# 64-token chunks, values scaled in place of keys, and a new order of all pieces in a fused RetNet and channel-mix kernel

## The chip, the cores and the metric

The kernel runs on one core of one Trainium2 chip. The metric is the device time of that core in microseconds (us), the median of several runs. The core's engines run side by side, each through its own queue in order: TensorE (PE in the profile, with its weight loads as PEld), VectorE (DVE), ScalarE (ACT), GpSimd (POOL) and SyncE (SP). DMAs are issued from SP, ACT and POOL; only those issued from POOL change the type on the way in this kernel.

## The reference

Four sequences of 768 tokens go through a recurrence with 8 heads of 64 channels, and its output x (512 channels) through an RWKV channel mix with a hidden width of 1024:

```python
gamma = 1.0 - 2.0 ** (-5.0 - np.arange(H))
for t in range(S):
    state = gamma[None, :, None, None] * state + np.einsum('bhd,bhe->bhde', k[:, :, t], v[:, :, t])
    y[:, :, t] = scale * np.einsum('bhd,bhde->bhe', q[:, :, t], state)
...
xk = mu_k * x + (1.0 - mu_k) * x_prev          # x_prev: x one token earlier
xr = mu_r * x + (1.0 - mu_r) * x_prev
k = np.maximum(xk @ w_k, 0.0)
v = k * k @ w_v
r = 1.0 / (1.0 + np.exp(-(xr @ w_r)))
return (r * v).astype(np.float32)
```

## The kernel before

A block is 256 tokens of one sequence; there are 12 blocks, three to a sequence (n = 0 to 11). The recurrence is computed in chunks of 128 tokens, two to a block. Within a block a chunk is held on 64 partitions, each with two neighbouring tokens (i = 0, 1), so one row of a load is 128 numbers of 4 bytes. The decay is taken out: keys are multiplied by powers of gamma (`scale_k`, L191, on DVE or POOL), scores are masked with a 0/1 matrix, and the result is multiplied by `gy` (`yout`, L343), a table that `powers` (L503, L506) makes.

Per block the pieces are: loads of k, q, v (L178; q and v are made 16-bit on the way); `ks`, the scaling of keys; T, Tq, Tk, the transposes on PE (L206, L224), and E, their copies out of PSUM on ACT (L252); S, the scores (L260), and M, the mask on DVE (L267, once for each i); C, the chunk's share of the state (L285); U, its sum with the decayed state (L297, L301), and G, the decay of that sum on POOL (L304); I and Y, the product of state and queries and that of scores and values (L316, L329); D, `gy` (L343, L351); dx, the difference of neighbouring tokens (L358, on DVE or POOL); X, the two mixes xk and xr, four pieces each (L372). Then K, the matmuls with w_k (L389, L409), with Q, relu and square on ACT (L397 to L419); R, the gate's matmuls (L423), and s, its sigmoid on ACT (L429); V, the matmuls with w_v (L435, the last block's second half in two parts, L453); O, the product (L441, L460); st, the store (L448). z are matmuls on zeros that fill PE's time at the start (L497).

The order is written out by hand or by a program, as one text of words, `ORDER`. A word is a piece with its numbers and, behind @, its PSUM banks; each engine gets its instructions in the order of the words. The framework puts in the waits. Buffers are rings of two to six tiles; a load waits until the last reader of the tile four blocks back has finished. In the first two blocks several pieces are split (Xu, du, Du, Ku work on 128 tokens).

```python
out=KS(n)[:, :, h0:h1], in0=K32(n)[:, h0:h1].rearrange("p h (i d) -> p i h d", i=2),
in1=gks[:, :, h0:h1, None].to_broadcast([P, 2, h1 - h0, D]), op=ALU.mult
```

Of the kernel before, what the change touches and what calls it, by code (L numbers as in the profile page):

```python
# [14 lines left out]
KSC = 64.0  # L15
ORDER = """
lk.0.0.2.4 lk.0.0.0.2 lq.0.0.2 lq.0.2.4 lv.0 lk.1.2 lq.1 ks.0.0.2.4 lv.1 wk.0 ks.0.0.0.2 gy z.12@1
T.0.1.0.2@0 wk.1 T.0.1.2.4@1 E.0.1.0.2 lk.2.2 mu z.2@4 Tq.0.2.4@23 Tq.0.0.2@45 E.0.0.0.2 E.0.1.2.4
z.3@6 S.0.0.0.2@45 C.0@67 M.0.0.0.2 E.0.0.2.4 U.0.0 z.1@0 S.0.0.2.4@23 M.0.0.2.4 I.0.0@45
S.0.1.0.2@01 ks.1.1 M.0.1.0.2 z.1@6 S.0.1.2.4@23 M.0.1.2.4 U.0.1 z.4@6 Y.0 G.0.1 Tq.1@67 Du.0.1  # L20
T.1.1@2 E.1.0 lq.2 Du.0.0 mt@3 wr me du.0.0.1 E.1.1 du.0.0.0 wv.0 Xu.0.1.1.1.2 z.6@0 S.1.0@23 lv.2
Xu.0.0.0.3.4 C.1@45 Xu.0.0.1.3.4 Xu.0.0.0.2.3 Xu.0.0.0.0.1 wv.1 Xu.0.0.1.1.2 Xu.0.0.0.1.2
Xu.0.1.1.0.1 lq.3 Xu.0.1.1.2.3 z.6@0 Ku.0.0.0@6 Xu.0.0.1.0.1 Xu.0.0.1.2.3 lk.3.2 Xu.0.1.1.3.4
Ku.0.1.0@7 Xu.0.1.0.2.3 Qu.0.0.0 U.1.0 M.1.0 G.1.0 Ku.0.0.1@4 Qu.0.1.0 ks.2.1 I.1.0@01 S.1.1@67
M.1.1 Tq.2@23 Xu.0.1.0.1.2 Y.1 E.2.0 Xu.0.1.0.3.4 U.1.1 T.2.1@6 Du.1.0 G.1.1 Qu.0.0.1 Ku.0.1.1@7
lk.4.2 du.1.0.0 R.0.1@0 Xu.0.1.0.0.1 Qu.0.1.1 lv.3 Xu.1.0.0.0.1 Xu.1.0.0.2.3 Xu.1.0.0.3.4 R.0.0@7
Xu.1.0.0.1.2 lv.4 E.2.1 Du.1.1 Ku.1.0.0@4 Xu.1.1.0.0.1 s.0.0 du.1.0.1 lq.4 V.0.1.0@1 Qu.1.0.0
Xu.1.1.0.1.2 Xu.1.1.1.0.1 Xu.1.1.0.2.3 lk.5.2 S.2.0@45 Xu.1.1.1.3.4 C.2@7 Xu.1.0.1.2.3
Xu.1.1.0.3.4 Ku.1.1.0@6 Xu.1.0.1.3.4 U.2.0 M.2.0 R.1.0@2 G.2.0 Qu.1.1.0 V.0.0.0@3 lv.5
Xu.1.1.1.2.3 s.0.1 s.1.0 I.2.0@45 S.2.1@67 V.0.0.1 M.2.1 V.0.1.1 Xu.1.0.1.0.1 Xu.1.0.1.1.2 ks.3.1  # L30
Y.2 O.0.1 Tq.3@67 O.0.0 Ku.1.0.1@2 D.2 lk.6.2 Ku.1.1.1@3 Qu.1.0.1 dx.2.0 lq.5 T.3.1@2 Qu.1.1.1
V.1.0.0@4 X.2.0.2.3 V.1.1.0@3 E.3.1 X.2.0.1.2 X.2.0.0.1 ks.4.0 V.1.0.1 E.3.0 C.3@01 Xu.1.1.1.1.2
lk.8 S.3.0@67 X.2.0.3.4 T.4.1@2 X.2.1.1.2 K.2.1@5 O.1.0 E.4.1 U.3.0 X.2.1.3.4 K.2.0@4 Q.2.1
X.2.1.0.1 X.2.1.2.3 R.1.1@5 U.3.1 Q.2.0 M.3.0 G.3.1 V.1.1.1 s.1.1 C.4@01 O.1.1 I.3.0@45 S.3.1@67
R.2.0@2 M.3.1 st.1.1 st.0.1 K.2.2@3 st.0.0 s.2.0 U.4.0 st.1.0 G.4.0 Tq.4@67 Y.3 ks.5.1 E.4.0 U.4.1
V.2.1.0@2 D.3 Q.2.2 S.4.0@67 I.4.0@01 dx.3.1 S.4.1@45 lk.9 M.4.0 K.2.3@3 M.4.1 R.2.1@6 Q.2.3 G.4.1
V.2.0.0@3 lq.6 X.3.1.0.1 s.2.1 X.3.1.1.2 V.2.0.1 X.3.0.3.4 lv.7 X.3.0.1.2 Tk.5@67 X.3.0.0.1 lq.7
Tq.5@45 X.3.1.3.4 E.5.1 V.2.1.1 X.3.1.2.3 lv.6 X.3.0.2.3 E.5.0 R.3.1@6 O.2.0 lq.8 O.2.1 C.5@3
S.5.0@45 U.5.0 Y.4 G.5.0 R.3.0@7 D.4 ks.6.1 K.3.3@3 s.3.0 M.5.0 s.3.1 K.3.1@2 Q.3.3 lv.8 dx.4.0
I.5.0@45 S.5.1@67 lk.7.2 Q.3.1 K.3.0@3 M.5.1 lq.9 K.3.2@2 Q.3.0 X.4.0.1.2 lk.10.2 ks.8.0 Tk.6@67  # L40
Y.5 Q.3.2 V.3.0.0@3 D.5 E.6.1 V.3.1.0@2 X.4.0.3.4 X.4.1.3.4 V.3.1.1 dx.5.0 C.6@67 Tq.7@45
X.4.1.2.3 Tq.6@01 X.4.0.0.1 E.7.0 V.3.0.1 X.4.0.2.3 X.4.1.1.2 E.6.0 K.4.2@4 U.6.0 O.3.0 K.4.0@6
X.4.1.0.1 Q.4.2 st.3.0 X.5.0.3.4 st.2.1 O.3.1 S.6.0@45 Tk.8@01 Q.4.0 X.5.1.1.2 st.3.1 K.4.1@3
X.5.0.1.2 E.8.1 X.5.1.2.3 R.4.0@6 X.5.0.0.1 X.5.1.3.4 X.5.0.2.3 K.4.3@2 s.4.0 X.5.1.0.1 Q.4.1
ks.7.0 K.5.1@6 Q.4.3 R.5.1@3 U.6.1 lk.11 M.6.0 G.6.1 st.2.0 V.4.0.0@7 s.5.1 ks.9.1 Q.5.1 V.4.0.1
Tk.7@45 O.4.0 I.6.0@23 S.6.1@01 E.7.1 K.5.2@6 M.6.1 C.7@45 Q.5.2 Y.6 U.7.0 S.7.0@67 G.7.0 D.6
Tq.8@01 V.4.1.0@4 E.8.0 lv.10 dx.6.0 V.4.1.1 lq.11 R.4.1@0 X.6.0.1.2 U.7.1 K.5.0@1 s.4.1 M.7.0
G.7.1 lq.10 K.5.3@0 Q.5.0 O.4.1 lv.9 X.6.0.2.3 Tq.9@67 I.7.0@45 Q.5.3 X.6.1.2.3 S.7.1@23 X.6.1.3.4
R.5.0@1 X.6.0.0.1 X.6.1.0.1 V.5.0.0@0 s.5.0 X.6.0.3.4 M.7.1 E.9.0 V.5.0.1 K.6.1@1 O.5.0 X.6.1.1.2
S.8.0@23 Q.6.1 Y.7 Tk.9@01 D.7 C.8@6 E.9.1 K.6.2@7 dx.7.0 R.6.1@4 K.6.3@5 X.7.0.3.4 X.7.1.0.1  # L50
R.6.0@0 Q.6.3 X.7.0.0.1 X.7.1.1.2 K.6.0@5 U.8.0 s.6.1 M.8.0 G.8.0 V.5.1.0@6 Q.6.0 ks.10.1 I.8.0@45
S.8.1@23 Q.6.2 V.5.1.1 M.8.1 s.6.0 lv.11 V.6.0.0@7 X.7.0.1.2 O.5.1 S.9.0@01 C.9@23 X.7.1.3.4
st.5.1 Y.8 X.7.1.2.3 st.5.0 X.7.0.2.3 st.4.1 V.6.0.1 U.9.0 st.4.0 D.8 K.7.3@2 M.9.0 dx.8.1 R.7.0@6
Q.7.3 V.6.1.0@2 O.6.0 s.7.0 U.9.1 I.9.0@01 S.9.1@67 G.9.1 K.7.0@3 M.9.1 K.7.1@4 Q.7.0 X.8.1.0.1
X.8.0.2.3 V.6.1.1 X.8.1.2.3 Q.7.1 X.8.1.1.2 Y.9 X.8.0.0.1 Tq.10@45 D.9 Tk.10@67 K.7.2@3 X.8.0.1.2
R.7.1@0 X.8.0.3.4 Q.7.2 dx.9.0 K.8.1@3 X.9.0.3.4 K.8.0@1 Q.8.1 X.9.1.1.2 X.8.1.3.4 V.7.1.0@3 O.6.1
E.10.0 V.7.1.1 X.9.1.2.3 st.6.1 X.9.0.2.3 Q.8.0 ks.11.0 K.8.2@2 E.10.1 V.7.0.0@1 X.9.0.0.1
X.9.0.1.2 s.7.1 V.7.0.1 Q.8.2 O.7.1 K.8.3@0 O.7.0 st.7.0 C.10@23 Q.8.3 S.10.0@67 st.7.1 U.10.0
Tk.11@45 st.6.0 M.10.0 Tq.11@01 G.10.0 V.8.0.0@2 E.11.0 U.10.1 E.11.1 I.10.0@67 G.10.1 S.10.1@01
R.8.0@3 M.10.1 V.8.1.0@4 s.8.0 X.9.1.3.4 X.9.1.0.1 C.11@3 S.11.0@01 U.11.0 Y.10 M.11.0 G.11.0  # L60
V.8.1.1 D.10 R.9.1@3 I.11.0@01 dx.10.1 s.9.1 S.11.1@67 K.9.1@5 M.11.1 R.8.1@3 Q.9.1 X.10.0.1.2
X.10.1.0.1 Y.11 s.8.1 X.10.1.1.2 X.10.0.3.4 R.9.0@5 X.10.1.3.4 X.10.0.2.3 K.9.0@3 X.10.1.2.3
X.10.0.0.1 K.9.2@6 Q.9.0 D.11 V.8.0.1 O.8.1 K.9.3@3 dx.11.0 K.10.3@4 X.11.1.1.2 K.10.0@7
X.11.1.3.4 X.11.0.2.3 X.11.0.1.2 V.9.1.0@0 Q.10.0 O.8.0 V.9.0.0@7 X.11.0.0.1 st.8.0 Q.9.3
X.11.0.3.4 X.11.1.2.3 R.10.1@1 X.11.1.0.1 Q.9.2 R.10.0@3 s.9.0 K.10.1@6 Q.10.3 V.9.1.1 s.10.1
K.10.2@2 Q.10.1 O.9.1 K.11.1@6 st.9.1 st.8.1 K.11.2@0 Q.11.1 V.10.1.0@6 Q.10.2 R.11.0@1 Q.11.2
V.10.1.1 s.10.0 K.11.3@0 O.10.1 s.11.0 K.11.0@3 st.10.1 V.10.0.0@1 Q.11.0 V.10.0.1 Q.11.3 V.9.0.1
O.10.0 V.11.0.0@6 st.10.0 O.9.0 V.11.0.1 st.9.0 R.11.1@7 O.11.0 st.11.0 Vc.11.1.0@6 s.11.1
Vc.11.1.1@7 Oc.11.1.0 sc.11.1.0.0 Oc.11.1.1 sc.11.1.1.1
# [4 lines left out]
def kernel(  # L74
# [17 lines left out]
    C = 128  # L92
    TM = 2 * C
# [6 lines left out]
    LOG = 7  # L100
# [3 lines left out]
    tok = 2 * (par % (P // 2))[:, None] + np.arange(2)[None, :]  # L104
    causal_np = (np.arange(C)[None, None, :] >= tok[:, :, None]).astype(np.float16)
    c16_np = np.concatenate([np.eye(P, dtype=np.float16), causal_np.reshape(P, -1)], axis=1)
    gk_np = gam[None, None, :] ** (C - 1 - tok[:, :, None])
    h_pj = 2 * np.arange(NJ)[None, :] + (par // D)[:, None]
    gd_np = gam[h_pj] ** C
    g0_np = 0.125 * KSC * gam[h_pj] ** (1 - C)  # L110
    pw_np = gam[h_pj][:, None, :] ** (2.0 ** np.arange(LOG)[None, :, None])
    small_np = np.concatenate(
        [x.reshape(P, -1) for x in (gk_np, gd_np, g0_np, pw_np, np.eye(P, 2 * NCO))], axis=1
    ).astype(np.float32)
    c16d = nc.inline_tensor(c16_np, name="c16")
    smalld = nc.inline_tensor(small_np, name="csmall")

# [9 lines left out]
    V16 = ring("v16_", 4, [H, 2 * D], F16)  # L127
    K32 = ring("k32_", 4, [H, 2 * D], F32)
    KS = ring("ks_", 3, [2, H, D], F16)
    QT = ring("qT_", 3, [NJ, 2, C], F16)  # L130
    KT = ring("kT_", 3, [NJ, 2, C], F16)
    A2 = ring("a2_", 3, [2, 2, NJ, C], F16)
    T32 = ring("t32_", 4, [NJ, D], F32)
    TG = ring("tg_", 6, [NJ, D], F16)
    DX = ring("dx_", 2, [NJ, TM], F32)
    XM = [ring("xk_", 3, [NJ, TM], F16), ring("xr_", 3, [NJ, TM], F16)]
    KR = ring("kr_", 2, [2, TM], F32)
    K2 = ring("k2_", 3, [NFO, TM], F16)
    RS = ring("rs_", 5, [dm], F32)
    OS = ring("os_", 5, [dm], F32)  # L140

    c16 = const.tile([P, 3 * P], F16, name="c16_sb")
    csm = const.tile([P, 2 * H + (2 + LOG) * NJ + 2 * NCO], F32, name="csm_sb")
    gy = const.tile([P, NJ, C], F32, name="gy_sb")
    zero = const.tile([P, 512], F16, name="zero")
    mu8 = const.tile([P, P], F32, name="mu8")
    mu = const.tile([P, 2 * NCO], F32, name="mu")
    wk16 = const.tile([P, NCO, dff], F16, name="wk16")
    wv16 = const.tile([P, NFO, dm], F16, name="wv16")
    wr16 = const.tile([P, NCO, dm], F16, name="wr16")  # L150
    xT = [const.tile([P, NJ, COLS], F32, name=f"xT{b}") for b in range(B)]
    ident = c16[:, 0:P]
    causal = c16[:, P:].rearrange("p (i t) -> p i t", i=2)
    o = 2 * H
    gks = csm[:, 0:o].rearrange("p (i h) -> p i h", i=2)
    gd = csm[:, o : o + NJ]
# [26 lines left out]
    def load_q(n, j0=0, j1=NJ):  # L183
        load(nc.gpsimd, q, Q16, n, j0, j1)
# [393 lines left out]
```

## Time and profile before

| | us |
|---|---|
| median of 3 runs | 159.01 (158.79 to 160.4) |
| span of the profiled execution | 157.6 |
| PE, DVE, ACT, POOL busy | 150.9, 124.7, 93.4, 61.6 |

The profile is one execution. Busy time is the time in which an engine works on at least one instruction; consecutive instructions overlap a little, so the sum of durations is larger. A matmul's duration holds about 0.2 us of pipeline that the next one overlaps, so how long a group occupies PE is read from the chain of waits or from the distance between starts. The DMA row of the page is the busy share of the 16 DMA engines in tenths, in 40 slices of 3.94 us.

### The profile page before, as it was taken

What the parts mean: (1) busy time and instruction counts of PE and PEld (TensorE: products, weight loads), DVE (VectorE), ACT (ScalarE), POOL (GpSimd) and SP (SyncE); (2) the same over time, 40 slices, a digit from 0 to 9 for tenths busy, and PEclk for the clock granted to TensorE, in tenths of its full rate; (3) what the DMA queues carried; (4) which work ended last, traced back from release to release, by engine and by line L of the source; (5) the groups of instructions that cost most, each with busy time, mean ns of one, the idle gap of its engine ahead of it and who ended that gap; (6) DMA issues with size and microseconds to landing.
All of it is one profiled execution on the core that took longest, in us unless ns stands there. A gap on an engine that the chain in (4) does not pass through costs nothing.

```text
span 157.6 us, 5995 instructions
## 1 busy us (share of the span) xinstructions
PE 150.9 (96%) x2676; PEld 97.5 (62%) x2676; DVE 124.7 (79%) x228; ACT 93.4 (59%) x149; POOL 61.6 (39%) x68
## 2 busy tenths in 40 slices
PE   6999889999999999999999999999999999999991
PEld 2446667567757558577567675666765667575550
DVE  0788969889987989999799888999988899811241
ACT  3235378618756539679966649155897143889710
POOL 7959768655018989200656007160003320000000
PEclk9999999999999999999999999999999999999998
DMA  5999999999996599965339900850015000112152
GB/s 138 211 219 207 258 205 198 245 244 240 256 206 235 141 172 170 238 160 204 93 111 135 135 4 6 110 227 4 25 41 204 4 4 0 67 58 75 71 198 69
DMA packets 36873, 22.01 MB, mean 140 GB/s; under 512 B 25832, under 2 KB 32880, under 8 KB 36848
## 3 DMA queue, kind: packets, MB, share of 16 engines
q0 software_dynamic: 28768, 13.11, 59.0%
q1 hardware_dynamic: 7632, 8.26, 15.3%
q8 instruction: 21, 0.34, 0.9%
q10 hardware_dynamic: 448, 0.26, 0.7%
q14 instruction: 4, 0.03, 0.1%
HBM read 24.25 MB, written 6.29 MB: 194 GB/s over the span
## 4 chain that ended last, share of the span: by engine, by line
PE 81%; DMA 7%; POOL 4%; ACT 4%; DVE 1%; issue 1%; DVEq 0%; POOLq 0%
PE ps L435 24%; PE ps L409 22%; PE ps L423 13%; DMA wk<-in_moe_w_k_dram 7%; PE ps L389 4%; PE ps L260 4%; PE ps L329 4%; PE ps L224 3%; PE ps L316 3%; PE ps L285 2%; ACT kr L416 2%; POOL q L178 2%; ACT k L419 1%; PE ps L453 1%; POOL v L178 1%
## 5 line engine op out<-in xcount | busy, mean ns | idle before, releaser
L435 PE MATMUL ps<-wv,k 128*128 128x512 f16 x184 | 44.6, 380 | 0.0
L409 PE MATMUL ps<-xk,wk 128*128 128x256 f16 x320 | 39.4, 273 | 0.2 <-ACT kr L416 0.2
L409 PEld LDWEIGHTS <-wk 128*128 128x128 f16 x320 | 30.5, 98 | 8.1 <-issue 0.5
L416 ACT ACTIVATE kr<-ps 128x512 f32<-128x512 f32 x40 | 23.7, 591 | 19.5 <-PE ps L409 19.5
L267 DVE TENSOR_TENSOR a<-ps,c_sb 128x1024 f16<-128x1024 f32 (+1 forms) x26 | 29.4, 1137 | 5.6 <-PE ps L260 5.5
L304 POOL TENSOR_TENSOR tg<-t,csm_sb 128x256 f16<-128x256 f32 x16 | 9.8, 613 | 53.1 <-DVE t L301 53.1
L435 PEld LDWEIGHTS <-k 128*128 128x128 f16 x184 | 17.0, 98 | 17.8 <-ACT k L419 0.4
L419 ACT ACTIVATE k<-kr 128x512 f16<-128x512 f32 x40 | 25.2, 630 | 1.3
L441 DVE SCALAR_TENSOR_TENSOR os<-ps,rs 128x512 f32<-128x512 f32 x23 | 15.5, 685 | 13.2 <-PE ps L435 8.5
L423 PE MATMUL ps<-wr,xr 128*128 128x512 f16 x96 | 24.4, 379 | 0.0
L372 DVE SCALAR_TENSOR_TENSOR xk<-dx,mu,xT 128x256 f16<-128x256 f32 (+1 forms) x56 | 23.1, 440 | 0.5 <-POOL dx L358 0.3
L372 DVE SCALAR_TENSOR_TENSOR xr<-dx,mu,xT 128x256 f16<-128x256 f32 (+1 forms) x56 | 23.1, 439 | 0.0
L429 ACT ACTIVATE rs<-ps 128x512 f32<-128x512 f32 x24 | 13.8, 588 | 13.0 <-PE ps L423 13.0
L252 ACT COPY qT<-ps 128x1024 f16<-128x1024 f16 (+1 forms) x13 | 12.2, 947 | 8.2 <-PE ps L224 8.2
L252 ACT COPY kT<-ps 128x1024 f16<-128x1024 f16 (+1 forms) x13 | 12.2, 942 | 6.1 <-PE ps L206 4.4
L191 POOL TENSOR_TENSOR ks<-k,csm_sb 128x1024 f16<-128x1024 f32 x7 | 13.3, 1899 | 3.5 <-DMA k<-in_k_dram 3.5
L423 PEld LDWEIGHTS <-xr 128*128 128x128 f16 x96 | 8.9, 98 | 8.4 <-DVE xk L372 0.2
L343 DVE TENSOR_TENSOR xT<-ps,gy_sb 128x1024 f32<-128x1024 f32 x10 | 12.2, 1220 | 1.8 <-PE ps L329 1.6
L497 PE MATMUL ps<-zero 128*128 128x512 f16 x35 | 11.2, 460 | 1.2 <-DVE xT L481 1.2
L178 POOL DMA_DIRECT2D q<-in_q_dram x13 | 11.7, 903 | 1.3 <-POOLq L562 0.8
L260 PE MATMUL ps<-qT,kT 64*64 64x128 f16 x384 | 11.7, 220 | 0.1
L358 DVE TENSOR_TENSOR dx<-xT 128x1024 f32<-128x1024 f32 (+1 forms) x11 | 11.2, 1026 | 0.2
(45 smaller groups left out, 155.5 us busy)
## 6 DMA issues: line engine op xcount, KB each, us to landing
out_dram<-os SPq DMA_DIRECT2D x23, 256.0 KB, 2.7
k<-in_k_dram POOLq DMA_DIRECT2D x8, 512.0 KB, 10.0
v<-in_v_dram POOLq DMA_DIRECT2D x12, 256.0 KB, 6.7
q<-in_q_dram POOLq DMA_DIRECT2D x11, 256.0 KB, 6.8
k<-in_k_dram SPq DMA_DIRECT2D x3, 512.0 KB, 4.5
wk<-in_moe_w_k_dram POOLq DMA_DIRECT2D x2, 512.0 KB, 10.5
wv<-in_moe_w_v_dram POOLq DMA_DIRECT2D x2, 512.0 KB, 13.2
k<-in_k_dram SPq DMA_DIRECT2D x2, 256.0 KB, 3.5
```

Of the source, the lines that this page charges most:

```text
L178: eng.dma_start(out=d(n)[:, 2 * j0 : 2 * j1], in_=rows(x, n)[:, 2 * j0 : 2 * j1])
L252: nc.scalar.copy(out=out, in_=pt)
L260: nc.tensor.matmul(pa[u * D : u * D + D, hp, j, :], lhsT=KT(n)[r, j, i, u * D : u * D + D], rhs=QT(n)[r, j, u, :], start=(j == j0), stop=( ...
L267: nc.vector.tensor_tensor(out=A2(n)[:, i, :, j0:j1], in0=pairs(banks("S", n, i, j0))[:, :, j0:j1], in1=causal[:, i, None, None, :].to_broa ...
L372: nc.vector.scalar_tensor_tensor(out=XM[w](n)[:, j, t0:t1], in0=DX(n)[:, j, t0:t1], scalar=mu[:, w * NCO + j : w * NCO + j + 1], in1=x[:, ...
L409: nc.tensor.matmul(pz[:, i, :], lhsT=wk16[:, co, fo * P : fo * P + P], rhs=XM[0](n)[:, co, :], start=(i == 0 and co == 0), stop=(co == NCO ...
L416: nc.scalar.activation(out=kr, in_=banks("K", n, g).rearrange("p (i t) -> p i t", i=2), func=AF.Relu)
L419: nc.scalar.activation(out=K2(n)[:, 2 * g : 2 * g + 2], in_=kr, func=AF.Square)
L423: nc.tensor.matmul(banks("R", n, tb), lhsT=XM[1](n)[:, co, tb * P : tb * P + P], rhs=wr16[:, co, :], start=(co == 0), stop=(co == NCO - 1),)
L429: nc.scalar.activation(out=RS(2 * n + tb), in_=banks("R", n, tb), func=AF.Sigmoid, scale=1.0 / KSC)
L435: nc.tensor.matmul(banks("V", n, tb, 0), lhsT=K2(n)[:, fo, tb * P : tb * P + P], rhs=wv16[:, fo, :], start=(fo == 0), stop=(fo == NFO - 1),)
L441: nc.vector.scalar_tensor_tensor(out=OS(2 * n + tb), in0=banks("V", n, tb, 0), scalar=1.0 / (KSC * KSC), in1=RS(2 * n + tb), op0=ALU.mult, ...
```

## The change

The chunk is 64 tokens everywhere, four to a block. A block's 256 tokens are two slots of 128, and a slot lies on 128 partitions, one token each. Per block, S and Y now have 32 matmuls of 64 columns each where they had 32 of 128, I has 32 of 64 columns (24 in the first block of a sequence) where it had 16 (8) of 128, and M is one DVE instruction for the block. C has 32 matmuls (24 in the last block of a sequence, before 16). U has four steps instead of two, each adding into the next; the first is a copy in the first block of a sequence. Keys are loaded as 16-bit and not scaled; values are loaded as 32-bit and scaled, on DVE for four blocks and half of block 0, and on ACT for the others, in 16 instructions a block of 64 columns, each with its own scale. Once a block (not a chunk) the state decays, on ACT in four instructions or on DVE in one. POOL issues loads and computes nothing. k and v come in two loads a block, one a slot, with rows of 64 numbers (256 bytes); q keeps its rows of 512 bytes, except in block 0. Block 0's first k, v and q come by SP as 32-bit; k and q are cast by DVE and ACT.

`gy` is read from memory for half and made on ACT for the other half. All transposes are the 64x64 form. D is two DVE instructions a block, dx is always on DVE. X covers two blocks at once for blocks 3 and 4, 6 and 7, 9 and 10 (`GROUPS`). Relu and square (Qa, Qb) are separate words over four buffers (two before). All words are in a new order. Core of the diff:

```diff
+GROUPS = ((0,), (1,), (2,), (3, 4), (5,), (6, 7), (8,), (9, 10), (11,))
...
+    W = 64
-    tok = 2 * (par % (P // 2))[:, None] + np.arange(2)[None, :]
+    tok = par[:, None] + P * np.arange(2)[None, :]
+    step_np = (np.arange(W)[None, :] >= (par % W)[:, None]).astype(np.float16)
...
+            for s in slots(i):
+                dst = staged(a, s) if (a, n, s) in EARLY else d(n)[:, :, s * D : s * D + D]
+                e.dma_start(out=dst, in_=src[:, s * P : s * P + P].rearrange("h p d -> p h d"))
...
+    def scale_v(e, n, i=None):
+        s = slots(i)
+        if e is nc.scalar:
+            for t in s:
+                for h in range(H):
+                    nc.scalar.activation(
+                        out=VS(n)[:, t, h], in_=V32(n)[:, h, t * D : t * D + D], func=AF.Copy,
+                        scale=gks[:, t, h : h + 1],
+                    )
+            return
...
+    def scores(e, n, i=None):
+        for j in range(NJ):
+            for k, s in enumerate(slots(i)):
+                for hp in range(2):
+                    a = side(j, hp)
+                    for u in range(2):
+                        nc.tensor.matmul(
+                            pa[low(u), a, j, k, :], lhsT=KT(n)[low(a), j, s, low(u)],
+                            rhs=QT(n)[low(a), j, s, low(u)],
...
+    def summed(e, n, c):
+        to = T32(n) if c == 3 else TG[c + 1](n)
+        if c == 0 and first(n):
+            copy(e, to, src)
+        else:
+            nc.vector.tensor_tensor(out=to, in0=src, in1=TG[c](n), op=ALU.add)
...
-T.1.1@2 E.1.0 lq.2 Du.0.0 mt@3 wr me du.0.0.1 E.1.1 du.0.0.0 wv.0 Xu.0.1.1.1.2 z.6@0 S.1.0@23 lv.2
+U.1.0 X.0.0.0.1 lv.2~p U.1.1 U.1.2 X.0.0.3.0 X.0.0.1.1 vs.2~a U.1.3 G.1~a z.4@4 I.1@01 S.1@67
```

In the new words the letter behind ~ is the engine (v DVE, a ACT, p POOL, s SP).

## The prediction

> **What bounds the kernel now.** I read the page's head first: which engine is full, and when.
>
> ```profile
> PE 150.9 (96%) x2676; PEld 97.5 (62%) x2676; DVE 124.7 (79%) x228; ACT 93.4 (59%) x149; POOL 61.6 (39%) x68
> ...
> DMA  5999999999996599965339900850015000112152
> ...
> PE 81%; DMA 7%; POOL 4%; ACT 4%; DVE 1%; issue 1%; DVEq 0%; POOLq 0%
> ```
>
> PE is busy 150.9 of 157.6 us; the DMA engines are full for the first 47 us and often until 70. The chain that ended last is 81% PE. Its DMA share is one piece, the wait for w_k. From the chain in order of time:
>
> ```profile
> 7.16 11.46 DMA wk<-in_moe_w_k_dram
> 18.66 1.96 PE ps L389 x32
> ...
> 54.32 0.64 PE ps L224 x64
> ...
> 63.24 0.38 PE ps L224 x32
> ...
> 66.98 0.38 PE ps L285 x32
> ...
> 70.71 0.35 PE ps L260 x16
> ...
> 125.03 0.34 PE ps L316 x8
> ...
> 127.78 0.45 PE ps L329 x28
> ```
>
> These are start, length and group, and they show what a small group costs PE's stream. The groups by shape give the engines beside it:
>
> ```profile
> L267 DVE TENSOR_TENSOR a<-ps,c_sb 128x1024 f16<-128x1024 f32 x22 | 26.7, 1218 | 4.7 <-PE ps L260 4.6
> L372 DVE SCALAR_TENSOR_TENSOR xk<-dx,mu,xT 128x256 f16<-128x256 f32 x40 | 18.4, 478 | 0.5 <-POOL dx L358 0.3
> L301 DVE TENSOR_TENSOR t<-ps,tg 128x256 f32<-128x256 f32 x16 | 6.7, 418 | 2.0 <-PE ps L285 1.3 <-POOL tg L304 0.7
> L358 DVE TENSOR_TENSOR dx<-xT 128x1024 f32<-128x1024 f32 x7 | 8.5, 1219 | 0.1
> ```
>
> So PE's amount of work sets the time, and the rest is hidden as long as it keeps up. As a check I added PE's pieces along the word order at the chain's prices: block 9's Y ends at 103 us of PE work and the whole at 148; in the trace these stand at about 108 and 154. Five us are lost, nearly all before 23 us, and the other 3.5 are the last store. The median is 1.4 above this span.
>
> **PE's pieces.** 64 transposes take 0.64 us where 32 take 0.38: a further 32 matmuls of 64x64 by 64 columns cost 0.26 (8.1 ns each) and entering a group 0.12. All attention pieces get that shape.
> - S: 16 of 128 columns cost 0.35 - 0.12 = 0.23, a block 0.46; now 0.26. Twelve blocks: -2.4.
> - Y: 28 in 0.45 - 0.12, so 0.38 for 32; now 0.26: -1.4.
> - I: 8 in 0.34 - 0.12, 27.5 ns each, 160 of them 4.4 us; now 352 at 8.1 ns, 2.9: -1.5.
> - C: 32 more: +0.3. Transposes: 40 of the 128-wide form (8 in 0.45, 2.2 us) and 224 small (1.8) become 384 small (3.1): -0.9.
> - Zeros: 33 for 35, 0.22 each: -0.4. K, R and V stream the same columns; groups of small pieces number 32 for 33. Nothing.
>
> Sum -6.3. One end: S and Y save nothing (-2.5); the other, the page's busy times per line (L260 11.7 and L329 9.3 against 5.9 for 384 transposes), about -9 for these two alone. I keep -6.3, the value from the stream itself.
>
> [...]
>
> **Waits that go.** PE waited 0.6 for w_k at 18.66; the new order runs eight K groups of blocks 0 and 1 on the first half of w_k before the second is needed. PE's L316 waited 0.8 in its weight loads for POOL's L304, which is gone; a third of it may have been hidden. Together -1.1; bounds -1.8 and 0, where DVE or ACT is late in POOL's place.
>
> **DVE** (by the spacing of starts, about 80 ns under the durations). M: 22 of 1.13 and 4 of 0.60 become 11 and 2: -13.7. U: 40 for 20, 0.34 each: +6.7; four decays, +1.3. dx: the seven of 1.13 become eleven, four halves two: +3.3. D: 24 halves of 0.60 for 10 of 1.13 and 4: +0.7. X: 8 of 0.26, 44 of 0.40, 24 of 512 columns at 0.66 (0.40 plus 256 times the 1.04 ns between the two shapes) for 32 and 80: -4.6. `gy` -1.9, three casts and copies +1.5, scaling -0.6. Sum -7: DVE does less than before, though its work comes earlier.
>
> **ACT** takes over 136 small instructions (120 for values, 16 decays). No such row exists. The square reads 128x512 from SBUF in 0.54 spacing; with 0.78 ns a column (the 1024-column copy's 0.89 less the sigmoid's 0.49) 64 columns come to 0.19. Without any overlap it is the 202 ns of the 128x1 activation plus 50, 0.255. I take 0.22, between two near ends: 30 us, for 93.4 before, plus 1.5 for `gy`, less 2 for copies that go to DVE. Queued behind 16 such pieces (3.5 us) stand the copies E and the relu Qa; C waits for the pieces, K's banks for Qa. Adding each engine's work along the new words up to block 9's Y, I get 84 us for PE, 82 for DVE and 86 for ACT. In the old order they stood at 103, 91 and 63. For two thirds of the run three engines are level, so some waits show: +0.5 taken, bounds 0 and +7 (below).
>
> [...]
>
> **Loads.** POOL's 28.8 us of arithmetic (L191, L304, L358) no longer stand in its queue, nor its 53 us of waiting for DVE's L301 ahead of loads. POOL issues 60 loads at 0.9 us, 54 us: hidden, POOL has nothing else. The transfers decide. In the trace, q and v loads queued from 53 to 60 us landed 1.45 us apart (512 KB, 1024 packets); the w_k and w_v halves landed 2.6 apart (1 MB, 512 packets). Solved for packets and bytes: 1024 packets 0.2 us, 512 KB 1.25. A half load of k or v has 1024 packets and 256 KB: 0.83. If packets alone counted, 1.45. A block then costs 1.45 + 4 x 0.83 = 4.8 (at most 7.25), 4.5 before. By the last transpose of keys: 3.5 for the first landing, 13 for weights, 12 x 4.8, 7 stores of 0.65: 79 us. PE comes to it after 76 of work and the 5 lost at the start, 81. So I take nothing for loads, but their cover is only 2 us; break-even is 0.87 a half load. The early SP loads (four of 256 KB, as much as 1.2 apart before) stand in for loads of the same bytes: nothing.
>
> [...]
>
> **Sum.** 157.6 - 6.3 - 1.1 + 0.5 = 150.7, and 1.4 to the median: 152.1, forecast 152.0. Start and last store are left as they are.
>
> **Rivals.**
> - *Loads become the bound; slower.* 256-byte packets cost nearly a 512-byte packet. In the profile: the DMA row is full while loads are queued, and most of q0's packets are small; against it: the solved prices. At price p the last load is 48(p - 0.87) us late, in a static order PE waits that long: 1.2 gives 152 + 16 = 168. It decides from 1.05, where the gain of 7 is eaten. 256-byte loads issued from SP may be slowest, and they open the kernel.
> - *ACT becomes the bound for the first two thirds.* At 0.24 its work to block 9 is 89 us plus 5 of start: 94 against PE's 89, time about 155; at 0.255, 157 to 159. For it: three engines level. Against: ACT stood idle for its own inputs most of the time, so any piece it gets early is free.
> - *The change doesn't do what it says on PE.* S and Y cost as before: -2.5 in place of -6.3, 155.8.
>
> **How the numbers follow.** Forecast 0.57; ACT 0.18; loads 0.18; PE pieces 0.07. A measurement of this kernel tells about 1% (1.6 us) from no change. The forecast's own range is 147.5 (PE's other end, waits all gone) to 157. Faster by over 1%, under 157.4: 0.55 + 0.12 + 0.05 = 0.72. Within: 0.02 + 0.04 + 0.02 and 0.01 from loads, 0.09. Slower, over 160.6: loads 0.17, ACT 0.02: 0.19. The range of 8 in 10 is 147 to 163: it takes in ACT's case and loads up to a price of 1.1.
>
> **What would show it.** PE busy near 143 to 145; S and Y groups of 32 near 0.26 to 0.38 us; M 11 times at 1.2; POOL's busy time all DMA issue; small ACT pieces near 0.22 apart. Wrong if PE shows idle time released by DMA of k or v (loads), by ACT's VS or E (ACT), or if half loads queued on POOL land over 1.0 us apart.

## The result, and the profile after

| | before | after |
|---|---|---|
| median (runs) | 159.16 us (158.79 to 160.4, 4) | 179.55 us (177.59 to 181.49, 4) |
| profiled span | 157.6 | 177.2 |
| ratio, 95% interval | | 1.121 [1.112, 1.129] |

The changed kernel is 12% slower, where 152 us was forecast. The ratio leaves out its slowest run, 181.49 us, in which the granted clock was lower than in the others (0.934 for 0.95). The page's head, of the changed kernel (busy time, 40 slices of 4.43 us, one DMA queue, the chain's shares):

```profile
PE 151.8 (86%) x2986; PEld 94.8 (54%) x2986; DVE 121.4 (69%) x212; ACT 123.2 (70%) x289; POOL 52.7 (30%) x64
...
PEclk9955896999999699999999999999999999999999
DMA  6999999999999934079992046010220003104143
...
q8 instruction: 23, 0.38, 0.9%
...
PE 52%; ACT 15%; DVE 14%; issue 9%; DMA 8%; DVEq 0%; ACTq 0%
```

PE is no busier than before (151.8 for 150.9 us), but the chain that ended last is 52% PE in place of 81%, and 9% of it is "issue": time in which an engine waited for nothing that the profile shows. Where the loss lies is told by stretches. Of before, then of after (start and end; length; then busy time and instructions of PE, PEld, DVE, ACT, POOL; granted clock; DMA share; GB/s):

```profile
0.00:20.00 20.00, 17.87 (x308) 10.01 (x309) 14.11 (x41) 7.10 (x12) 16.29 (x23) 1.00 1.27 206
20.00:40.00 20.00, 19.26 (x376) 13.03 (x372) 17.46 (x36) 12.92 (x21) 12.55 (x13) 1.00 1.43 227
40.00:60.00 20.00, 19.96 (x435) 12.84 (x435) 17.62 (x31) 11.40 (x18) 12.10 (x12) 1.00 1.09 199
60.00:80.00 20.00, 20.00 (x443) 13.75 (x444) 18.74 (x30) 16.68 (x27) 6.33 (x7) 1.00 0.91 183
```

```profile
0.00:20.00 20.00, 13.08 (x205) 6.25 (x205) 7.53 (x20) 10.01 (x34) 13.86 (x20) 0.74 1.33 192
20.00:40.00 20.00, 16.30 (x496) 11.37 (x495) 14.95 (x33) 14.90 (x39) 13.64 (x17) 0.91 1.60 204
40.00:60.00 20.00, 15.36 (x360) 9.94 (x364) 13.64 (x24) 15.24 (x31) 13.77 (x16) 0.92 1.69 216
60.00:80.00 20.00, 19.64 (x522) 12.62 (x515) 18.94 (x29) 17.07 (x47) 3.31 (x4) 0.99 0.52 105
```

In the first 60 us PE is busy 57.1 us before and 44.7 after, at a lower granted clock, while the DMA engines are full in both. Yet the number of matmuls it gets through is about the same: 1119 and 1061. PE after the change, in order of time (start, length, group; in brackets the idle time ahead and what ended it):

```profile
48.63 0.45 PE L286 MATMUL ps<-qT,kT 64*64 64x64 f16 x32
48.90 0.22 PE L351 MATMUL ps<-qT,tg 64*64 64x64 f16 x4
51.55 0.25 PE L351 MATMUL ps<-qT,tg 64*64 64x64 f16 x7 [2.43 <-issue]
...
53.27 0.46 PE L254 MATMUL ps<-c_sb,k 64*64 64x64 f16 x32
53.55 0.34 PE L368 MATMUL ps<-a,vs 64*64 64x64 f16 x16
56.10 0.32 PE L368 MATMUL ps<-a,vs 64*64 64x64 f16 x16 [2.21 <-issue]
```

I and Y stop in the middle of a group whose inputs are all there. There are eight such stops of over 0.4 us. I counted PE's instructions from the first (each matmul and each weight load is one): the eight stand at instructions 705, 1217, 1729, 1985, 3265, 3521, 3777 and 4545, all of the form 193 + 256k. The 23 packets of queue q8 are 16,384 bytes each, 64 bytes for each of 256 instructions. Their number is that of the boundaries passed, so I pair them in order: the packet that starts behind one boundary is the one whose end PE waits for at the next. In the trace of after, while loads are queued, such a packet starts 3.7 us (median of the first eight) after PE has passed a boundary, takes 1.0 us, and at each of the eight stops PE goes on 1.2 to 1.6 us after its end. In before the delay is 3.8 us up to 46 us, and 0.7 us after 76 us, when few loads are left. So while POOL's loads were queued, 256 PE instructions took about 6 us (3.7 + 1.0 + 1.2 to 1.6), however short they were; the stretches that ended in a stop took 4.4 to 7.3 us, as the delay was shorter or longer. The kernel before lay just inside this: its stretches of 256 took 6.1 to 6.9 us up to 67 us, with no gap over 0.25.

That these packets bring PE's instructions, 256 at a time, is read from their queue's name in the profile ("instruction") and from their number: 21 packets for the 21 boundaries in the 5359 instructions of before, 23 for 23 after the change, 20 for 20 in e1, 25 for 25 in e3, 22 for 22 in e14. I call such a transfer a fetch.

This gives one number that compares all kernels here, where PE's instruction 2241 stands: 60.8 us before, 62.5 after. PE keeps the same pace in instructions, but by then it has done 50.0 us of work before and 32.5 after (each matmul at its undisturbed distance of starts: 8.5 ns for 64x64 with 64 columns, 18 with 128 columns; 109 and 216 for the wide ones). That is 17.5 us less work done, and the span is 19.6 longer. PE's whole span by the same prices, every gap over 0.25 us put down to what ended it:

| us | before | after |
|---|---|---|
| work | 138.6 | 130.3 |
| gaps at 193 + 256k, or one instruction later | 0.0 | 13.2 |
| gaps ended by ACT | 0.6 | 4.5 |
| gaps ended by DVE | 1.0 | 4.1 |
| gaps ended by DMA; by nothing seen elsewhere | 1.2; 0.0 | 1.7; 1.6 |
| shorter losses, slower clock among them | 11.1 | 16.8 |
| ahead of the first and from the last matmul on | 5.0 | 4.8 |

Part of the shorter losses lies where the granted clock is low. After the change the granted clock is 0.50 in three stretches, 9.2 to 19.4, 26.3 to 29.7 and 57.0 to 60.4 us (the 5s and 6s in the row PEclk). Of the 16.8 us of shorter losses 4.6 lie in them, and 12.2 elsewhere, about as much as before. The first lies among PE's waits for DMA, ACT and DVE at the start; the other two begin right behind the stops that end at 25.9 and 56.1 us, and hold 2.4 of the 4.6.

### The profile page after: what moved, and what is told of

Read it like the earlier page. It is cut to its first block, busy times and chain, and to the rows that moved or that the text cites. A ratio compares the mean times of both kernels' runs of the same rounds, so it can differ in the third digit from the quotient of the medians.

```text
span 177.2 us, 6759 instructions
## 1 busy us (share of the span) xinstructions
PE 151.8 (86%) x2986; PEld 94.8 (54%) x2986; DVE 121.4 (69%) x212; ACT 123.2 (70%) x289; POOL 52.7 (30%) x64
## 4 chain that ended last, share of the span: by engine, by line
PE 52%; ACT 15%; DVE 14%; issue 9%; DMA 8%; DVEq 0%; ACTq 0%
PE ps L446 18%; PE ps L483 11%; PE ps L471 11%; ACT vs L230 8%; DMA v<-in_v_dram 6%; ACT kr L455 3%; DVE xk L432 3%; DVE dx L403 3%; PE ps L254 3%; DVE a L303 2%; PE ps L312 2%; DVE os L489 2%; DVE xr L432 2%; PE ps L548 2%; PE ps L351 2%
## 5 line engine op out<-in xcount | busy, mean ns | idle before, releaser
L446 PE MATMUL ps<-xk,wk 128*128 128x256 f16 (+1 forms) x416 | 47.8, 266 | 4.4 <-issue 3.6
L483 PE MATMUL ps<-wv,k 128*128 128x512 f16 x184 | 44.7, 380 | 0.0
L446 PEld LDWEIGHTS <-wk 128*128 128x128 f16 x416 | 37.5, 99 | 13.4 <-issue 4.7
L230 ACT ACTIVATE vs<-v,csm_sb 128x64 f16<-128x64 f32 x120 | 29.4, 337 | 2.3 <-DMA v<-in_v_dram 2.3
L209 POOL DMA_DIRECT2D k<-in_k_dram x23 | 20.5, 904 | 22.7 <-PE ps L254 18.8
L483 PEld LDWEIGHTS <-k 128*128 128x128 f16 x184 | 17.2, 98 | 17.5
L209 POOL DMA_DIRECT2D v<-in_v_dram x20 | 18.0, 914 | 7.9 <-ACT kr L455 3.6
L432 DVE SCALAR_TENSOR_TENSOR xk<-dx,mu,xT 128x256 f16<-128x256 f32 (+2 forms) x40 | 19.9, 532 | 0.2
L432 DVE SCALAR_TENSOR_TENSOR xr<-dx,mu,xT 128x256 f16<-128x256 f32 (+1 forms) x36 | 19.6, 566 | 0.1
L388 DVE TENSOR_TENSOR xT<-ps,gy_sb 128x512 f32<-128x512 f32 x22 | 15.2, 689 | 5.5 <-PE ps L351 4.0
L303 DVE TENSOR_TENSOR a<-ps,c_sb 128x1024 f16<-128x1024 f32 (+1 forms) x13 | 14.8, 1138 | 5.7 <-PE ps L286 4.6
L215 ACT COPY qT<-ps 128x1024 f16<-128x1024 f16 (+1 forms) x12 | 11.7, 974 | 8.0 <-PE ps L254 7.7
L328 DVE TENSOR_TENSOR tg<-ps,tg 128x256 f16<-128x256 f32 x32 | 13.5, 421 | 5.1 <-PE ps L312 3.8
L471 PEld LDWEIGHTS <-xr 128*128 128x128 f16 x96 | 9.2, 100 | 11.5 <-issue 2.5
L312 PE MATMUL ps<-vs,k 64*64 64x64 f16 x352 | 8.9, 198 | 5.9 <-DVE vs L236 3.0
## 6 DMA issues: line engine op xcount, KB each, us to landing
wk<-in_moe_w_k_dram POOLq DMA_DIRECT2D x2, 512.0 KB, 11.5
wr<-in_moe_w_r_dram POOLq DMA_DIRECT2D x1, 512.0 KB, 11.3
```

The lines of the kernel that those rows point to most:

```text
L209: e.dma_start(out=dst, in_=src[:, s * P : s * P + P].rearrange("h p d -> p h d"))
L230: nc.scalar.activation(out=VS(n)[:, t, h], in_=V32(n)[:, h, t * D : t * D + D], func=AF.Copy, scale=gks[:, t, h : h + 1],)
L303: nc.vector.tensor_tensor(out=out, in0=ps, in1=mask, op=ALU.mult)
L432: nc.vector.scalar_tensor_tensor(out=XM[w](k)[:, j, t0:t1], in0=DX(k)[:, j, t0:t1], scalar=mu[:, w * NCO + j : w * NCO + j + 1], in1=x[:, ...
L446: nc.tensor.matmul(pz[:, i, :], lhsT=wk16[:, co, fo * P : fo * P + P], rhs=XM[0](k)[:, co, m * TM + t0 : m * TM + t1], start=(i == 0 and c ...
L471: nc.tensor.matmul(banks("R", n, tb), lhsT=XM[1](k)[:, co, t : t + P], rhs=wr16[:, co, :], start=(co == 0), stop=(co == NCO - 1),)
```

## The experiments

Theory 1 in every expectation is PE's instruction stream. The other numbers are rivals: loads whose data comes late, ACT's small pieces as the bound, or what the expectation names. The table gathers what is read from each run: the time is its median, beside 159.1 to 160.2 us for the kernel before on the same chips; the last four columns are from one profile each. The last column is PE's idle time alone, without the part of a gap that the end of the matmul before it covers, so it has 11.7 where the table above has 13.2; where a gap is taken to begin moves it by up to 0.4.

| | time, us | PE instructions | 2241 passed at | work by then | gaps over 0.25 at 193 + 256k |
|---|---|---|---|---|---|
| before | 159.2 | 5359 | 60.8 | 50.0 | 0.0 |
| after | 179.6 | 5983 | 62.5 | 32.5 | 11.7 |
| e1_wide_t | 175.8 | 5215 | 68.6 | 42.4 | 5.4 |
| e2_loads_once | 170.9 | 5981 | 58.1 | 32.5 | 4.4 |
| e3_dup_t | 181.3 | 6575 | 60.4 | 45.4 | 10.0 |
| e4_vs_copy | 177.0 | 5983 | 60.6 | 32.5 | 9.7 |
| e5_wide_zeros | 165.9 | 5439 | 61.0 | 50.8 | 0.2 |
| e6_late_loads | 174.3 | 5359 | 60.4 | 50.0 | 0.5 |
| e7_early_v | 180.2 | 5983 | 61.3 | 32.5 | 12.1 |
| e8_early_wide | 170.5 | 5215 | 63.3 | 42.4 | 4.9 |
| e9_unread | 177.1 | 5981 | 62.5 | 32.5 | 8.3 |
| e10_v_by_sp | 178.9 | 5215 | 73.0 | 42.4 | 8.2 |
| e11_paced4 | 177.9 | 5983 | 56.4 | 32.5 | 8.0 |
| e12_paced6 | 176.1 | 5983 | 56.1 | 32.5 | 9.9 |
| e13_wide_paced6 | 170.8 | 5215 | 65.3 | 42.4 | 4.5 |
| e14_mixed_paced6 | 173.5 | 5599 | 63.8 | 42.1 | 6.7 |

**Fewer instructions for the same transposes.** e1 takes the changed kernel and makes each group of 32 small transposes 16 of 128 rows:

```diff
-                    for u in range(2):
-                        for hp in range(2):
-                            nc.tensor.transpose(pt[low(side(j, hp)), u, j, k, :],
-                                src[low(u), 2 * j + hp, s * D : s * D + D], ident[low(u), low(u)])
+                    for hp in range(2):
+                        nc.tensor.transpose(pt[low(side(j, hp)), j, k, :],
+                            src[:, 2 * j + hp, s * D : s * D + D], ident)
```

> The changed kernel with its transposes done as 16 matmuls of 128 rows by 128 columns each instead of 32 of 64 by 64 (same loads, same result, 768 fewer PE instructions counting weight loads, 5205 for 5973). Theory 1 (PE's instruction stream): PE fetches its instructions in pieces of 256 over the same DMA engines, and while loads are queued a piece is there only some 5.5 us after the one before was begun, so PE stalls where 256 instructions run faster; the stalls just ahead of every 256th instruction (13 us in all in the changed kernel) fall to 3 to 8 us, against 2 to 5 us more of PE work: 5 us less to 1 us more than 179. Theory 2 (loads late by their packets) and theory 3 (ACT too slow): nothing falls, PE's work comes on top: 181 to 184.

175.8 us, ratio to before 1.099 [1.091, 1.108]. A group takes 0.57 us in place of 0.27, which for 24 groups is 7 us more of PE's time (4 us by the price of the matmuls alone, 134.5 for 130.3), and the kernel is still 3.7 us faster: gaps at the boundaries fall from 11.7 to 5.4 us.

**The loads left out.** In e2 the loads of blocks 4 to 11 are left out, and these blocks are computed from what blocks 0 to 3 left:

```diff
         def go(e, n, i=None):
+            if n >= 4:
+                return
```

> The changed kernel without the loads of k, q and v of blocks 4 to 11, which then compute on the data of blocks 0 to 3. Theory 1 (instruction stream): the DMA engines are idle from about 45 us, the stalls ahead of every 256th instruction after that (9.7 us of the 13) shrink to under 2 us and the clock dip behind them goes (2 us): 167 to 170. Theory 2 (loads late): the same time, but then the waits that go are waits released by DMA of k, q or v, at any instruction, and the stalls at every 256th stay. Theory 3 (ACT): 176 to 179.

170.9 us, 8.7 less, at the edge of the 167 to 170 that theory 1 gave. The gaps that remain (26.6, 33.1, 39.0, 53.3 us) lie in or just behind the stretch in which loads run; those at 83 to 110 are gone. This alone doesn't tell queue from data; e9 does. And e2 is still 10.9 us slower than the kernel before on the same chip, though its gaps at the boundaries are down to 4.4 us: by the prices of the table above its gaps ended by ACT are 7.6 us (4.5 after the change) and those ended by DVE 4.2. The instruction stream is the largest part of the loss, but not all of it.

**The same loss put into the kernel before.** e3 does each small transpose twice, e5 adds the same PE time as two wide matmuls on zeros ahead of each of these groups:

```diff
# e3
-        for j in range(j0, j1):
+        for j, _ in [(j, x) for x in range(2) for j in range(j0, j1)]:
# e5
+        for u, w in ((0, 512), (1, 128)):
+            nc.tensor.matmul(banks("T", n, a, j0)[:, u, 0:w], lhsT=zero[:, 0:P], rhs=zero[:, 0:w], ...)
```

> The kernel before with every small transpose done twice into the same place (1216 more PE instructions, same result, nothing else moved). At the price of PE's stream, 0.26 us for 32 matmuls, 19 groups cost 5 us: 164, which theories 2 and 3 expect. Theory 1: in the first 65 us, where loads are queued, 256 instructions took 6.1 to 6.7 us and a piece is not there sooner than some 5.5; the groups there come faster than the pieces, stalls appear ahead of every 256th instruction that the kernel before does not have: 167 to 172.

> The kernel before, with two matmuls on zeros (512 and 128 columns, 0.27 us by the prices of the trace) ahead of each of the 19 groups of small transposes: as much PE work as the doubled transposes of e3_dup_t (+5.1 us), at the same places, but 38 matmuls in place of 608. Theory 1 (the instruction stream: 256 PE instructions can't come faster than about 6 us while loads are queued): only the work shows, 163 to 166 us, and the gaps at PE instructions 193 + 256k stay under 1 us in sum. Theory 2 (the order is tight: any PE work at these places pushes the engines apart): as e3_dup_t, 175 us and more, with waits for other engines. A result between 168 and 174 would speak for neither alone.

e3 took 181.3 us (1.134 [1.130, 1.137]), e5 165.9 (1.039 [1.028, 1.050]). Both added about 5 us of PE work (5.2 and 5.5 by the prices); against the kernel before on the same chip e5 lost 6.4 us and e3 21.3, more than the 167 to 172 us that theory 1 gave for it. Of the 21.3, 5.2 are the work, 11.8 the stops (by the distance of starts), and about 6 are shorter losses in three stretches of granted clock 0.50, each beginning in a stop or within 1.5 us of its end (at 27.3, 78.5 and 139.9 us). PE in e3, in order of time:

```profile
75.45 0.40 PE L285 MATMUL ps<-v,ks 64*64 64x64 f16 x25 [1.28 <-issue]
75.66 1.11 PE L224 MATMUL ps<-c_sb,q 64*64 64x64 f16 x103
79.45 0.58 PE L224 MATMUL ps<-c_sb,q 64*64 64x64 f16 x25 [2.68 <-issue]
```

PE runs 128 transposes, stops 2.7 us before the last 25, and goes on: instruction 3265. The waits of PE in e5 (group, what it waited for; us in total, times, longest) hold one entry of "issue", and it is small:

```profile
PE ps L503 <- DVE xT L487: 1.2, 1, 1.2
PE ps L206 <- DVE ks L191: 0.6, 1, 0.6
...
PE ps L415 <- issue: 0.2, 1, 0.2
```

So it is the number of instructions, not PE's time: the same work in 40 matmuls costs about what it weighs, in 608 four times that. One of e3's gaps (2.5 us at 138.5) lies where no load is queued: there 255 instructions were through in 1.2 us, and even with the queues nearly empty the stretch took 3.7.

**ACT's small pieces.** e4 replaces the 16 scaled pieces a block by one ACT copy; the values stay unscaled, which leaves out the decay's share in them:

```diff
+            s = slice(s[0], s[-1] + 1)
+            nc.scalar.copy(out=VS(n)[:, s], in_=V32(n).rearrange("p h (i d) -> p i h d", i=2)[:, s])
+            return
```

> The changed kernel with the values that ACT scales copied by ACT in one instruction a block, without their scale (the result is not the reference's): 120 ACT pieces of 0.245 us (29 us) become 8 of about 0.9. Theory 3 (ACT's small pieces hold PE up): the time falls by 8 to 15 us, to 165 to 171. Theory 1 and 2: C waits less in a few places, 1 to 4 us, 175 to 178, and the stalls at every 256th instruction stay near 13.

177.0 us (173.9 and 180.1). ACT loses 21.5 us of busy time on this line (29.4 to 7.9), and the gaps at the boundaries stay (9.7 us): ACT's pieces are not the main loss. That they cost nothing is not shown. The two runs lie too far apart, and the faster one is 3.7 us below the fastest of the changed kernel (177.6).

**The start.** In the changed kernel C's second half of block 0 waits 3.2 us for v. The chain of waits of the changed kernel, from 10 us on:

```profile
2.96 11.22 DMA v<-in_v_dram
14.18 0.02 issue
14.20 0.70 DVE vs L236
14.90 0.04 issue
14.95 0.48 PE ps L312 x12
```

SP's fourth load was issued at 3 us and landed at 14.2, beside POOL's. e7 moves it to the head of POOL's loads; e8 adds to that e1's transposes and sets k of block 9 ahead of block 10's:

```diff
- lk.0.0~s ... Ek.0.0~v lk.0.1~p mu vs.0.0~a C.0.0@23 ... lv.0.1~s vs.0.1~v
+ lk.0.0~s ... Ek.0.0~v lv.0.1~p lk.0.1~p mu vs.0.0~a C.0.0@23 ... vs.0.1~v
```

> The changed kernel, with block 0's second half load of v issued by POOL as its first load instead of by SP as its fourth. Theory of the start: the wait of C's second half of block 0 (3.18 us in the profile) falls under 1 us, and the whole becomes 2 to 3 us faster, 175 to 178 us against 179.5; the span 174 to 176. Rival: the other first loads are late anyway (the second half of k now lands later by one load), and the wait only changes its place: 179 to 181.

> The changed kernel with the early half load of e7_early_v, the transposes of e1_wide_t (16 matmuls for 32) and k of block 9 loaded ahead of k of block 10. If the start and the instruction stream are separate terms, their gains add: 172 to 174 us (e1_wide_t took 175.8). If an earlier start only meets the instruction stream earlier, 175 to 177.

e7 took 180.2 us (178.1 and 182.2), no gain; the span is 0.9 shorter. The waits of PE in e7:

```profile
PE ps L286 <- issue: 3.7, 1, 3.7
PE ps L446 <- issue: 3.5, 2, 2.7
PE ps L368 <- issue: 2.1, 1, 2.1
```

The wait for values is gone, and PE meets the stream earlier: instruction 705 now has a gap of 3.9 us at 24.4, where it was 2.0 at 25.9. With a thinner stream the same edit counts: e8 is at 170.5 us (1.068 [1.054, 1.082]), 5.3 below e1, and no variant with all its work done is faster in the median. It doesn't beat the kernel before. How much of the 5.3 is block 9's load was not told apart.

**Queue or data.** e9 brings e2's loads back, by POOL, into four spare tiles that nothing reads; e6 adds 48 such loads to the kernel before, by SP, behind its stores:

```diff
# e9
+            if n >= 4:
+                for s in range(2):
+                    nc.gpsimd.dma_start(out=spare[next(turn) % 4], in_=src[:, s * P : s * P + P]...)
+                return
# e6
+            nc.sync.dma_start(out=spare[i % 5], in_=v[i % B, :, t0 : t0 + P, :]...)
```

> The changed kernel, whose loads of k, q and v of blocks 4 to 11 (48 halves, issued by POOL and made 16-bit on the way) go into four spare tiles that nothing reads; those blocks are computed from what blocks 0 to 3 left, so the output is not that of the inputs. Against e2_loads_once (170.9 us), the same without these loads, only the transfers come back, not a wait for their data. Theory 1: between 45 and 95 us the stretches of 256 PE instructions that took 3.4 to 4.9 us in e2_loads_once grow to 5.5 and more, with gaps of 0.6 to 2.5 us at 193 + 256k at four boundaries or more: 176 to 182 us. Rival (what e2_loads_once gained were waits for data that comes late): 170 to 172.

> The kernel before, with 48 more loads of 256 KB of values in 256-byte packets, issued by SP behind its stores (8 after 71.5 us, 16 after 76, 16 after 101, 8 after 118) into tiles that nothing reads. No PE instruction is added. Theory 1: the stretches of 256 PE instructions that took 4.0 us (to 83.1), 4.2 (to 108.3) and 4.7 (to 122.6) in the trace of before grow to 5.5 to 6.3, with gaps at the boundaries: 162 to 166 us. Theory 2 (loads only cost where their data is late, and nothing reads this data): 159 to 161. If queues fed by SP leave the instruction fetch free, theory 1 gives 159 to 161 as well, and the times from a boundary to its fetch show which.

e9 took 177.1 us, 6.2 more than e2, though nobody waits for these transfers: gaps of 1.4 us at 51.6, 2.4 at 56.1 (0.8 in e2) and 1.5 at 84.0. Three boundaries, not the four expected. With at most four loads under way the fetch started 1.5 us after a boundary (median), so fewer stretches were caught.

e6 went another way. It took 174.3 us, but the stretches of 256 stayed at 4.0, 4.2 and 4.7 us. PE in e6, in order of time, and the group of the product:

```profile
92.31 0.31 PE L316 MATMUL ps<-qT,tg 64*64 64x128 f16 x2 [6.24 <-DVE os L441]
```

```profile
L441 DVE SCALAR_TENSOR_TENSOR os<-ps,rs 128x512 f32<-128x512 f32 x23 | 15.5, 686 | 27.5 <-DMA out_dram<-os 10.6
```

The idle loads stood ahead of stores in SP's queue, O waited for its output tiles (10.6 us), and PE for O. That loss has nothing to do with the fetch, which started 1.7 us after a boundary (median), less than the 3.7 behind the changed kernel's POOL loads. This doesn't tell the queue from how much stands in it: most of the idle loads landed 4 to 6 us after their issue and were issued about 1.2 us apart, so some four were under way, and with four of POOL's under way e9 has 1.5.

**Which queue.** e10 takes e8 and lets SP issue the loads of v of blocks 1 to 10.

```diff
-lv.1~p ... lv.10~p
+lv.1~s ... lv.10~s
```

> The kernel of e8_early_wide with the loads of v of blocks 1 to 10 issued by SP instead of POOL (32-bit on both sides, so nothing is converted). In e6_late_loads loads from SP let the instruction fetch start 0.2 to 2.2 us after a boundary, where POOL's made it 3.6. If POOL's queue is what holds the fetch, the gaps at 193 + 256k fall from 4.9 us to under 2.5 and the time from 170.5 to 166 to 169. If any queued transfer holds it, or SP's 256-byte loads land late beside POOL's as at the start (11 us) so that values come late, 170 to 175.

178.9 us, 8.4 slower than e8, a miss for the theory that only POOL's queue counts. With both queues full the fetch started 4.9 us after a boundary (median of seven, 3.9 to 6.8), stretches that ended in a gap took 6.2 to 8.1 us, and weights came late. DMA issues of e10 (us to landing at the end of a line):

```profile
wk<-in_moe_w_k_dram POOLq DMA_DIRECT2D x2, 512.0 KB, 17.9
...
wr<-in_moe_w_r_dram POOLq DMA_DIRECT2D x1, 512.0 KB, 23.4
```

After the change these were 11.5 and 11.3. The delays so far are 0.7 us with little queued (before), 1.7 behind SP's loads (e6), 3.7 behind POOL's (after) and 4.9 behind both (e10). The runs don't separate the number of full queues from the number of loads under way, and behind POOL's queue alone the delay depends on the latter, as the next two runs show.

**Fewer loads under way.** e11 and e12 leave PE as it is in the changed kernel (with e8's two moves of loads) and let POOL read one number of an older load's tile before it issues the next:

```diff
+            if len(under_way) >= DEEP:
+                old = under_way.pop(0)
+                e.tensor_copy(out=tick[0:1, 0:1], in_=old[0:1, 0, 0:1])
+            under_way.append(out)
```

> The changed kernel with the early half load of e7_early_v and k of block 9 ahead of block 10's, and POOL paced: before it issues a load it reads one number of the tile that its fourth load back fills, so at most four of its loads are under way (about eight in the profile of the changed kernel). No PE instruction is added or left out. In e9_unread, with four under way after 45 us, the fetch began 0.8 to 3.0 us after a boundary instead of 3.6. If the fetch waits behind POOL's queue, 256 instructions can come in 4 to 5 us, the gaps at 193 + 256k fall from 12.1 us (e7_early_v) to 2 to 5, and the time from 180 to 166 to 172. If four are too few to keep the transfers going (1.3 us for each half load in e9_unread, 0.85 in the changed kernel), data comes late: waits of PE released by DMA or by the scaling of values, and 173 to 185. If the fetch doesn't care how much is queued: gaps as they were, 177 to 181.

> As e11_paced4 with six loads under way. If the fetch waits behind the queue, the delay after a boundary lies between that of four and that of eight, and so does the sum of the gaps (5 to 9 us): 170 to 176 us, unless four starve the transfers; then six are the faster of the two.

The fetch started 2.6 and 3.0 us after a boundary (medians up to 70 us; 3.5 in e7 by the same count), and instruction 2241 came at 56.4 and 56.1 us, 5 us earlier than in e7: with no PE instruction changed, a shorter queue alone moves the pace. Part of that reached the end: 177.9 us for four (span 175.7), 176.1 for six (174.1 and 178.1; span 172.0, 4.3 shorter than e7). The waits of PE with four under way:

```profile
PE ps L266 <- DMA q<-in_q_dram: 4.3, 1, 4.3
PE ps L380 <- issue: 2.5, 1, 2.5
PE ps L298 <- issue: 1.9, 1, 1.9
```

Four starve the transfers, as the expectation feared: q of a later block is 4.3 us late at 93 us. Six don't, but behind 70 us, where the order is dense, its gaps are what they were in e7 (4.6 and 4.7 us).

**Both remedies.** e13 is e8 with six under way, e14 the same with the small transposes again from block 6 on (`pick` takes the wide form for n < 6).

> e8_early_wide (fewer PE instructions in the transposes, the early half load) with POOL paced to six loads under way as in e12_paced6. If the instruction stream is what is left, the gaps at 193 + 256k fall from 4.9 us to 1 to 3 and the time from 170.5 to 166 to 169. If the two remedies are the same gain twice, or other waits take the place, 170 to 173.

> As e13_wide_paced6, but with the 32 small transposes again in blocks 6 to 11: 12 groups at 0.27 in place of 0.57 us, 3.6 us less PE work, and 384 more PE instructions of which most fall between 65 and 110 us, where loads are still queued part of the time. If the fetch is quick enough there, 2 to 4 us faster than e13_wide_paced6; if not, gaps come back at 74 to 105 us (4.5 us of them in e12_paced6) and the two are equal within 1 us.

e13 took 169.4 and 172.2 us, with the profile from the slower one; e14 173.5. The gains don't add: e8 had 169.9 and 171.2. e14 got gaps back instead of time (70, 80, 90 us), as its second case said, and came out 2.7 us slower than e13, where that case expected them equal within 1. PE in e13:

```profile
47.69 1.04 PE L482 MATMUL ps<-wr,xr 128*128 128x512 f16 x4
51.23 1.37 PE L482 MATMUL ps<-wr,xr 128*128 128x512 f16 x4 [2.50 <-issue]
```

The fetch behind this stop started 4.4 us after its boundary (44.5), the one before it 6.3 us after 35.8, with the two halves of w_v, issued at 35.8 and 36.7 us, beside it. That six loads are no fixed amount when two of them hold 512 KB each would explain it; it was not tried.

## Why the prediction was wrong

The step that failed is the pricing of PE's pieces by their time alone ("a further 32 matmuls of 64x64 by 64 columns cost 0.26 (8.1 ns each) and entering a group 0.12"), with no term for how many instructions there are. The runs showed 13.2 us of stops in its place. The change adds 624 PE instructions (5983 for 5359), and shrinks the time of those it keeps, so that the early part of the order holds 32.5 us of work in 2241 instructions instead of 50.0. The trace of before showed the limit, without a gap: nine stretches of 256 in a row at 6.1 to 6.9 us, and 21 packets on an instruction queue. The prediction used neither.

By the table of gaps, the 19.6 us of span are: work -8.3, stops at the boundaries +13.2, gaps ended by ACT +3.9 and by DVE +3.1, the other gaps +2.1, shorter losses +5.7 (4.6 of them at half clock). So a second step failed as well, though it is smaller: +0.5 was taken for waits for ACT and DVE, and they grew by 7.0, of which 3.2 are the wait for scaled values at the start. Term by term:

- **PE's pieces, -6.3:** the mechanism was right and the gain larger, -8.3 (138.6 to 130.3). Groups of 32 take 0.26 to 0.28 us, as priced. PE busy at 143 to 145 didn't come (151.8); from 26.3 to 29.7 us, at a granted clock of 0.50, PE is busy all 3.4 us for 1.6 us of work by the prices.
- **Waits that go, -1.1:** those for w_k and for POOL's decay are gone, as forecast.
- **DVE, -7:** 3.3 us less busy (124.7 to 121.4), about half; the mask came 11 times whole and twice halved, 1.14 us in the mean, as forecast. PE's gaps ended by DVE are 4.1 us, 3.2 of them the wait for scaled values at the start; the chain that ended last still gives DVE 14% of the span.
- **ACT, 0.22 a piece:** 0.245 in the trace of after (3.92 us for 16), between the prediction's ends of 0.19 and 0.255. No row of before shows the 0.24 that the ACT rival took; it gave about 155 us, against 179.6 measured. Waits for ACT grew by 3.9 us, where 0.5 was taken for all waits. The chain that ended last gives these pieces 8% of the span; e4 shows that they are not the main loss, and leaves open whether they cost some us. The group, and the mask beside it:

```profile
L230 ACT ACTIVATE vs<-v,csm_sb 128x64 f16<-128x64 f32 x120 | 29.4, 337 | 2.3 <-DMA v<-in_v_dram 2.3
...
L303 DVE TENSOR_TENSOR a<-ps,c_sb 128x1024 f16<-128x1024 f32 (+1 forms) x13 | 14.8, 1138 | 5.7 <-PE ps L286 4.6
```

- **Loads, 0.83 for a half load, nothing taken:** the price held about (from 20 to 64 us the halves landed 0.87 us apart in the median, 0.5 to 1.6), and PE did not wait for their data after the start. "So I take nothing for loads" failed all the same: in e9 transfers that nobody waited for cost 6.2 us, with stops of 1.4, 2.4 and 1.5 us at boundaries. The rival "loads become the bound" gave 168 us by a price of 1.2 that never came; that it lies on the right side is no merit of its mechanism.
- **"Start and last store are left as they are":** wrong for the start. SP's fourth load, in packets of 256 bytes beside POOL's loads, took 11.2 us to land, which cost 3.2 us at C. In e7 only 0.9 us of span came back, because the stream was the next thing to be late.

What stays open: whether the number of full queues adds to the fetch's delay beside the loads under way; what ACT's pieces cost; why pacing and thinning together gave nothing over thinning; and why runs of the changed kernel differ by 2%. An order of words that spreads small matmuls between K, V and R, at most 256 instructions in 6 us, was not tried.

## What to carry to other kernels

Count PE's instructions, not only its time: here, while loads were queued, 256 matmuls and weight loads took about 6 us (6.1 to 6.9 before, 4.4 to 7.3 in the stretches of after that ended in a stop), so I would mix small matmuls with wide ones in the order. In these traces the sign was a gap in the middle of a group, ended by "issue", at instruction 193 + 256k, and the packets of queue q8 showed when each fetch started and how long it took (1.0 us). Before cutting a matmul into smaller ones, look at how long each 256 instructions take in the profile you have.

## What was not expected of the hardware

- PE's instructions came in pieces of 16,384 bytes (queue q8, 0.9% of the 16 DMA engines' span before and after): 1.0 us a piece, started 0.7 us after a boundary when little was queued (before), 2.6 with four of POOL's loads under way (e11), 3.7 with POOL's loads unpaced (after), 4.9 with POOL's and SP's (e10, up to 6.8).
- PE's granted clock fell to 0.50 for 3.4 us behind two of the eight stops, and for 10.2 us among the waits at the start; in the kernel before it was 1.00 in both places.
- A 256 KB load from SP in 256-byte packets, beside POOL's loads, landed after 11.2 us.
